# Norm work moved from VectorE to ScalarE and GpSimd, the projection's load on another queue, and a replanned order of the attention stage

## The chip, the cores and the metric

The kernel runs on one core of a Trainium2 chip. Its engines are TensorE (PE, matmuls, with PEld for its weight loads), VectorE (DVE), ScalarE (ACT), GpSimd (POOL) and SyncE (SP, which only issues transfers). ACT and POOL can issue transfers too. Each engine works through its own instructions in order and waits on semaphores for the others. The metric is device time in microseconds (us), the median of several runs; lower is better.

## What is computed

Three stages follow one another. Attention runs over 2 batches of 8 heads, 768 positions and 64 dimensions, with a mask from hash buckets: a query sees the keys whose six projected signs are its own. Its output, as 1536 tokens of 512, goes through a first gated layer of 1536 hidden units behind an RMS norm, and then through a second layer in which each token is sent to one of 8 experts.

```python
q_bits = (np.einsum('bhsd,dk->bhsk', q, proj) > 0)        # k_bits likewise
mask = q_bucket[:, :, :, None] == k_bucket[:, :, None, :]
scores = np.where(mask, scale * np.matmul(q, k.transpose(0, 1, 3, 2)), -1e9)
attn = softmax(scores)
x = np.matmul(attn, v)                                    # to 1536 tokens x 512
rms = np.sqrt(np.mean(x * x, axis=-1, keepdims=True) + 1e-06)
g = (x / rms * rms_g) @ w_gate
x = (silu(g) * ((x / rms * rms_g) @ w_val)) @ w_out
...                                                       # then one of 8 experts per token
```

## The kernel before, in words

**Attention** (to about 232 us of the profiled execution) goes over 8 pairs of heads, i = 0 to 7; j = 0 or 1 is the head in the pair. For each pair the raw k and q are transposed on PE (L660), split into a high and a low half HL (L669 on ACT, L682 on DVE) and projected with PRJ (`ph`, `pb`, L691 and L701). PRJ is made on DVE (step `prj`) from pj, the projection. For each of 12 blocks x of a pair (6 blocks of 128 keys for each head) there are four steps: `sm` on PE (L755) and `sx`, the row maximum on DVE (L763), for the mask; `sc`, the scores on PE (L806); `ex`, the exponential on ACT (L814, tile Pe); `pl`, the low half of it (L825, tile Pl), on POOL or DVE. Then come `pv` (L841 to L843, six query blocks of 18 short matmuls for each head), `pu` (L829, what unmatched queries get, which reads VB and UT, made by POOL at L928 and L780) and `ho` on DVE, three closing steps that write the head's output into X (L852, L856, L858). X holds the tokens, X_71 batch 0 and X_72 batch 1.

The order of all this is written out by hand: ORDER is five strings, one each for PE, ACT, DVE, POOL and SP, in which each word is a step. A class Plan plays the steps, each engine strictly in the order of its string, and gives them their buffers. Other steps stand in the same strings: `iz` clears the operand T of PE's warm-up matmuls (L588; the warm-up, L596, is the first thing PE does, in step `cols`), `rows` writes the mask's constants (L564 to L578), `prz` clears PRJ, `vm1` and `nid` derive small tiles from the identity ident, `z` clears the other T (L600), `n0` to `n5` are the norm of the first chunk and `w0` converts the first weights.

**The first layer** (232 to 560 us) works in three chunks of 512 tokens. Its 36 weight blocks, 12 each of gate (g), value (v) and output (o), come as 64-bit floats. The first chunk converts each of them: loaded into wraw (SP), rebiased on ACT (L439, tile hm), then shift, join and sign on DVE (L443, L447, L455), which gives wy. After that each use needs a high half on ACT (L473: wgh, wvh, woh) and a low half on POOL (L1165) or, for the first two, on DVE (L951). g0 and v0, the first blocks, are converted while attention still runs. A planner with costs orders this stage.

**The norm** of a chunk has 4 sums of squares (L362, 128x512 with an accumulated sum), then 19 operations on 128x4 tiles that find the inverse root (L369 to L392: a shift, a first guess, four Newton rounds of square, times, factor, better), and then the scaling (L399), all on DVE. The norm of chunk 0 runs in attention's pair 5, those of chunks 1 and 2 in the first layer; chunk 1 has tokens of both batches.

## Time and profile before

| | us |
|---|---|
| median of 3 runs | 775.87 |
| lowest, highest | 774.86, 778.15 |
| the profiled execution | 777.31 |
| its span, first to last instruction | 775.6 |

In the profiled execution PE was busy for 735.8 us of the span (95%), DVE for 464.5 (60%), POOL for 427.6 (55%) and ACT for 379.0 (49%). These shares are averages over the three stages, so they are to be read by stretches. In a timeline row the first number is the start in us from the span's beginning, the second the time that the row's instructions took together; brackets give how long the engine was idle before and what it then waited for.

### The profile page before, as it was taken

How to read it: one execution, taken by the hardware profiler on the slowest of the kernel's cores; microseconds unless marked ns; L12 is line 12 of the kernel's file. 1: busy time of each engine (PE TensorE's matmuls, PEld its weight loads, DVE VectorE, ACT ScalarE, POOL GpSimd, SP SyncE). 2: the span in 40 equal slices, each digit the busy share in tenths (PEclk: the TensorE clock that was granted, in tenths of full speed). 3: DMA queues.
4: the chain of work that ended last, by engine and by line, in shares of the span. 5: the costliest groups of instructions: out<-in, count | busy, mean ns of one | idle time of the engine just before them, and what ended most of it. 6: DMA issues, size and time to landing. Idle time of an engine off the chain costs nothing.

```text
span 775.6 us, 14106 instructions
## 1 busy us (share of the span) xinstructions
PE 735.8 (95%) x5349; PEld 618.7 (80%) x5349; DVE 464.5 (60%) x869; ACT 379.0 (49%) x615; POOL 427.6 (55%) x380
## 2 busy tenths in 40 slices
PE   6899999989997999999999999999959999999995
PEld 4678888878885688888887888888858989888894
DVE  5887777889888987786554225422344444464441
ACT  3566356546555444444434443443225666655662
POOL 4889988757773333335434443462155656645552
PEclk9999999999998999999999999999969999999998
DMA  6998785565214344540100010100369997767000
GB/s 130 197 195 171 151 171 116 104 135 116 71 53 139 93 144 144 162 138 27 54 2 1 1 55 0 32 24 0 123 190 326 337 283 225 216 176 180 24 25 21
DMA packets 109193, 92.17 MB, mean 119 GB/s; under 512 B 45663, under 2 KB 90809, under 8 KB 109122
## 3 DMA queue, kind: packets, MB, share of 16 engines
q1 hardware_dynamic: 103930, 82.29, 41.0%
q0 software_dynamic: 2560, 7.34, 3.1%
q10 hardware_dynamic: 2632, 1.60, 1.0%
q8 instruction: 43, 0.70, 0.4%
q14 instruction: 28, 0.23, 0.1%
HBM read 66.36 MB, written 7.36 MB: 95 GB/s over the span
## 4 chain that ended last, share of the span: by engine, by line
PE 83%; DVE 5%; DMA 3%; issue 3%; POOL 2%; ACT 2%; SPq 0%; ACTq 0%; POOLq 0%
PE pg L1146 23%; PE pg L1626 11%; PE pss L806 8%; PE po L1200 4%; PE po L1202 4%; PE po L1201 4%; PE psm L755 4%; PE po L1640 4%; PE po L1638 3%; PE po L1639 3%; PE po L841 2%; PE po L842 2%; PE po L843 2%; PE pt L346 1%; PE pt L660 1%
## 5 line engine op out<-in xcount | busy, mean ns | idle before, releaser
L825 POOL TENSOR_TENSOR Pl<-Pe 128x768 f16<-128x768 f32 x90 | 133.6, 1504 | 33.6 <-ACT Pe L814 31.9
L463 POOL TENSOR_TENSOR wgl<-r,wgh 128x512 fp32r<-128x512 f32 x64 | 83.9, 1317 | 79.6 <-ACT wgh L473 74.1
L814 ACT ACTIVATE Pe<-pss,ebias 128x768 f32<-128x768 f32 x96 | 85.0, 902 | 70.7 <-PE pss L806 49.8
L763 DVE TENSOR_REDUCE m<-psm 128x1 f32<-128x768 f32 x96 | 89.7, 952 | 22.9 <-PE psm L755 21.4
L806 PE MATMUL pss<-T 128*128 128x256 f32 (+1 forms) x384 | 83.9, 351 | 5.3 <-DVE m L763 2.9
L1165 POOL TENSOR_TENSOR wol<-wy_o,woh 128x512 fp32r<-128x512 f32 x36 | 48.4, 1345 | 68.4 <-ACT woh L473 68.4
L1165 POOL TENSOR_TENSOR wgl<-wy_g,wgh 128x512 fp32r<-128x512 f32 x29 | 38.8, 1338 | 78.1 <-ACT wgh L473 70.9
L806 PEld LDWEIGHTS pss<-T 128*128 128x128 f32 x384 | 64.6, 191 | 20.7 <-DVE m L763 3.4
L463 DVE TENSOR_TENSOR wvl<-r,wvh 128x512 fp32r<-128x512 f32 x64 | 47.2, 738 | 48.0 <-ACT wvh L473 45.9
L1626 PE MATMUL pg<-xh,wgh 128*128 128x256 f32 x256 | 73.3, 287 | 0.7 <-ACT xh L349 0.7
L1626 PE MATMUL pg<-xl,wgh 128*128 128x256 f32 x256 | 72.5, 283 | 0.0
L1626 PE MATMUL pg<-xh,wgl 128*128 128x256 f32 x256 | 72.5, 283 | 0.0
L1178 DVE TENSOR_TENSOR si<-pg,si 128x512 f32<-128x512 f32 x30 | 20.7, 688 | 83.1 <-PE pg L1146 83.1
L1146 PE MATMUL pg<-xh,wgh 128*128 128x512 f32 x144 | 58.1, 403 | 4.2 <-ACT wgh L473 3.5
L473 ACT CAST wgh<-r 128x512 fp32r<-128x512 f32 x64 | 39.7, 620 | 42.0 <-PE pg L1626 29.5
L1200 PE MATMUL po<-woh,hh 128*128 128x512 f32 (+1 forms) x148 | 58.8, 398 | 0.5 <-ACT yt L1214 0.5
L841 PE MATMUL po<-VS,Pe 128*128 128x65 f16 x576 | 58.8, 195 | 0.0
L843 PE MATMUL po<-VS,Pl 128*128 128x65 f16 x576 | 57.9, 193 | 0.9 <-POOL Pl L825 0.9
L1146 PE MATMUL pg<-xh,wgl 128*128 128x512 f32 x144 | 57.3, 398 | 1.5 <-POOL wgl L1165 1.2
L842 PE MATMUL po<-VS,Pe 128*128 128x65 f16 x576 | 58.2, 194 | 0.0
L1631 DVE SCALAR_TENSOR_TENSOR ehl<-pg,ehh 128x256 fp32r<-128x256 f32 x64 | 27.1, 424 | 51.6 <-ACT ehh L1630 51.6
L1146 PE MATMUL pg<-xl,wgh 128*128 128x512 f32 x144 | 57.7, 401 | 0.2 <-DVE xl L353 0.2
(260 smaller groups left out, 2021.8 us busy)
## 6 DMA issues: line engine op xcount, KB each, us to landing
r<-in_moe_w_dram SPq DMA_DIRECT2D x128, 256.0 KB
T<-HL SPq DMA_DIRECT2D x44, 384.0 KB
wraw<-in_moe_w_val_dram SPq DMA_DIRECT2D x12, 512.0 KB
wraw<-in_moe_w_gate_dram SPq DMA_DIRECT2D x12, 512.0 KB
wraw<-in_moe_w_out_dram SPq DMA_DIRECT2D x12, 512.0 KB
X<-in_v_dram SPq DMA_DIRECT2D x16, 192.0 KB
y_dram<-yt SPq DMA_DIRECT2D x12, 256.0 KB
kraw<-in_k_dram SPq DMA_DIRECT2D x15, 192.0 KB
```

What stands on the lines that cost most here:

```text
L463: eng.tensor_tensor(out=lo, in0=y, in1=r32(hi), op=ALU.subtract)
L763: v_.tensor_reduce(out=d["m", j][:, t:t + 1], in_=d.pop(("pm", n)), axis=AX.X, op=ALU.max)
L806: nc.tensor.matmul(pss[:, c], Tj[:, a, 0, ks], Tj[:, a, 1, c], start=a == 0, stop=a == 1)
L814: nc.scalar.activation(d["p", j][0][:, kb], d.pop(("s", n)), AF.Exp, bias=ebias, scale=1.0 / math.sqrt(D))
L825: eng.tensor_tensor(out=Pl[:, kb], in0=Pe[:, kb], in1=leading(Pe, kb), op=ALU.subtract)
L841: nc.tensor.matmul(po, leading(Pe, kb)[:, ts], vf[:, 0], start=t == 0 and kb == 0, stop=False, skip_group_check=True)
L842: nc.tensor.matmul(po, leading(Pe, kb)[:, ts], vf[:, 1], start=False, stop=False, skip_group_check=True)
L843: nc.tensor.matmul(po, Pl[:, kb, ts], vf[:, 0], start=False, stop=False, skip_group_check=True)
L1146: nc.tensor.matmul(pg, w_[:, dsl], x_[:, d], start=n == 0, stop=n == 3 * KD - 1)
L1165: nc.gpsimd.tensor_tensor(out=lo, in0=Y[(f, kind)], in1=r32(hi), op=ALU.subtract)
L1200: nc.tensor.matmul(pos[c, t][:, cols], d["hh"][:, tsl], wh[:, cols], start=first, stop=split, skip_group_check=split)
L1626: nc.tensor.matmul(ph, w_[:, dsl], x_[:, d], start=n == 0, stop=n == 3 * KD - 1)
```

## The change

1. `norm_sum`: the sum of squares of each 128x512 tile is an ACT activation (Square with accumulation) in place of a DVE operation; 4 for each of three chunks.
2. `norm_rsqrt`: 14 operations on POOL in place of 19 on DVE. The shift is folded into the guess (a multiplication by -0.5), and there are three Newton rounds in place of four.
3. pj, the projection's load: two transfers of 64x6 from POOL's queue, one ahead of and one behind the mask operation that makes the identity, in place of one of 128x6 from ACT's queue.
4. The first clears on DVE: `iz` first, then `rows`, `prz`, `bc`, `prj`; `vm1` and `nid` behind them.
5. o0 and g1 are also converted while attention runs, as g0 and v0 were (EARLY); the ring of converted weights is two shorter, and wraw and hm have a counted room in the plan.
6. All five strings of ORDER are new.

The diff, cut to its core (of ORDER only the first rows for DVE and POOL are shown):

```diff
-RING = 34
+RING = 32
...
-    "vm1 rows iz nid prz prj td.0.k bc td.0.q bh.0.1.0 bh.0.0.0 bh.0.0.1 bh.0.1.1 sx.0.0 sx.0.5 sx.0.2 sx.0.3 sx.0.1 sx.0.4 vx.0.0 mz.0.0 bi.1 sx.0.6 "
+    "iz rows prz bc prj td.0.k vm1 nid td.0.q bh.0.0.0 bh.0.1.0 bh.0.0.1 bh.0.1.1 sx.0.0 vx.0.0 sx.0.4 sx.0.2 sx.0.3 sx.0.5 sx.0.1 vx.0.2 mz.0.0 bi.1 "
...
-    "z.0.1 c1.0.0.0 ut0 zz z.0.0 z.1.1 z.1.0 c1.0.1.1 sv.0.1 ev.0 c1.0.1.0 c1.0.0.1 sv.0.2 ev.1 const sv.0.0 sv.0.3 pl.0.2 mk.0.0.3 pl.0.0 pl.0.4 pl.0.3 "
+    "pj z.0.1 z.0.0 c1.0.1.0 c1.0.0.1 ut0 c1.0.1.1 zz z.1.0 sv.0.0 sv.0.1 c1.0.0.0 const z.1.1 ev.0 sv.0.2 sv.0.3 pl.0.0 pl.0.3 pl.0.2 pl.0.5 pl.0.4 ev.1 "
...
     def norm_sum(c, i, sq, ss):
         xt = norm_tile(c, i)
-        v_.scalar_tensor_tensor(out=sq, in0=xt, scalar=1.0, in1=xt, op0=ALU.mult, op1=ALU.mult,
-                                accum_out=ss[:, i:i + 1])
+        nc.scalar.activation(sq, xt, AF.Square, accum_out=ss[:, i:i + 1])
 
     def norm_rsqrt(pool, d):
 
         def first():
             d["ms"] = pool.tile([P, CT], F32, name="nms")
-            v_.tensor_scalar(out=d["ms"], in0=d["ss"], scalar1=1.0 / DM, scalar2=1e-6, op0=ALU.mult, op1=ALU.add)
-
-        def half():
-            d["rb"] = pool.tile([P, CT], I32, name="nrb")
-            v_.tensor_scalar(out=d["rb"], in0=d["ms"].bitcast(I32), scalar1=1, scalar2=None, op0=ALU.logical_shift_right)
+            nc.gpsimd.tensor_scalar(out=d["ms"], in0=d["ss"], scalar1=1.0 / DM, scalar2=1e-6, op0=ALU.mult, op1=ALU.add)
 
         def guess():
             d["ri"] = pool.tile([P, CT], F32, name="nri")
-            v_.tensor_scalar(out=d["ri"].bitcast(I32), in0=d["rb"], scalar1=-1.0, scalar2=float(0x5F3759DF),
-                             op0=ALU.mult, op1=ALU.add)
+            nc.gpsimd.tensor_scalar(out=d["ri"].bitcast(I32), in0=d["ms"].bitcast(I32), scalar1=-0.5, scalar2=float(0x5F3759DF),
+                                    op0=ALU.mult, op1=ALU.add)
 
         def square():
             d["t1"] = pool.tile([P, CT], F32, name="nt1")
-            v_.tensor_tensor(out=d["t1"], in0=d["ri"], in1=d["ri"], op=ALU.mult)
+            nc.gpsimd.tensor_tensor(out=d["t1"], in0=d["ri"], in1=d["ri"], op=ALU.mult)
 
         def times():
-            v_.tensor_tensor(out=d["t1"], in0=d["t1"], in1=d["ms"], op=ALU.mult)
+            nc.gpsimd.tensor_tensor(out=d["t1"], in0=d["t1"], in1=d["ms"], op=ALU.mult)
 
         def factor():
-            v_.tensor_scalar(out=d["t1"], in0=d["t1"], scalar1=-0.5, scalar2=1.5, op0=ALU.mult, op1=ALU.add)
+            nc.gpsimd.tensor_scalar(out=d["t1"], in0=d["t1"], scalar1=-0.5, scalar2=1.5, op0=ALU.mult, op1=ALU.add)
 
         def better():
             ro = pool.tile([P, CT], F32, name="nri")
-            v_.tensor_tensor(out=ro, in0=d["ri"], in1=d["t1"], op=ALU.mult)
+            nc.gpsimd.tensor_tensor(out=ro, in0=d["ri"], in1=d["t1"], op=ALU.mult)
             d["ri"] = ro
 
-        return [first, half, guess] + [square, times, factor, better] * 4
+        return [first, guess] + [square, times, factor, better] * 3
 
...
+    EARLY = ((0, "g"), (0, "v"), (0, "o"), (1, "g"))
...
-            if f == 0 and kind != "o":
-                y = wa.tile([P, DM], F32, name=f"wy_{kind}0", bufs=1)
+            if (f, kind) in EARLY:
+                y = wa.tile([P, DM], F32, name=f"wy_{kind}{f}", bufs=1)
             else:
...
-                     "M": 2, "MK": 2}, ORDER)
+                     "M": 2, "MK": 2, "WR": 3, "TMP": 3}, ORDER)
...
         def load_pj():
-            nc.scalar.dma_start(pj[:, 0], proj.unsqueeze(0).to_broadcast((2, D, NB)))
+            for j in range(2):
+                nc.gpsimd.dma_start(pj[64 * j:64 * j + 64, 0], proj)
...
-        add(ACT, 620, "pj", load_pj, (), (), -1999, bw=-1500)
-        add(DVE, 170, "iz", idle_zero, (), (), -1000)
+        add(POOL, 1300, "pj", load_pj, (), (), -1999, bw=-2000)
+        add(DVE, 270, "iz", idle_zero, (), (), -1000)
         add(POOL, 900, "zz", max_zero, (), [("z", 0, 1)], -90)
-        add(DVE, 325, "prz", lambda: v_.memset(r32(PRJ), 0.0), (), (), -98)
+        add(DVE, 485, "prz", lambda: v_.memset(r32(PRJ), 0.0), (), ["iz"], -98)
         add(DVE, 2400, "prj", prj, (), ["pj", "prz"], -97, lock=True)
-        add(DVE, 120, "nid", lambda: v_.tensor_scalar(out=nident, in0=ident, scalar1=-1.0, scalar2=None, op0=ALU.mult), (), (), -90, lock=True)
-        add(DVE, 1200, "rows", mask_rows, (), (), -99)
-        add(PE, 580, "cols", mask_cols, (), ("rows", "iz"), -99, "V")
+        add(DVE, 120, "nid", lambda: v_.tensor_scalar(out=nident, in0=ident, scalar1=-1.0, scalar2=None, op0=ALU.mult), (), ["prj"], -90, lock=True)
+        add(DVE, 1200, "rows", mask_rows, (), ["iz"], -99)
+        add(PE, 1150, "cols", mask_cols, (), ("rows", "iz"), -99, "V")
         add(DVE, 150, "bc", lambda: v_.tensor_copy(bc, st[0].pop("pc")[:, 0:2]), (), ("cols",), -99, "", "V")
...
-            add(DVE, 760, ("n0", i), norm0_sum, (i,), done, N0 + N1 * i, "J", "J", lock=True)
+            add(ACT, 860, ("n0", i), norm0_sum, (i,), done, N0 + N1 * i, "J", "J")
         for n, f in enumerate(steps):
-            add(DVE, 163, ("n1", n), f, (), [("n1", n - 1)] if n else [("n0", i) for i in range(CT)], N0 + N1 * CT, lock=True)
+            add(POOL, 170, ("n1", n), f, (), [("n1", n - 1)] if n else [("n0", i) for i in range(CT)], N0 + N1 * CT)
...
-        for kind in "gv":
-            w = convert(0, kind)
+        for n, (c, kind) in enumerate(((0, "g"), (0, "v"), (0, "o"), (1, "g"))):
+            w = convert(c, kind)
             for m, (e, ns, f, args) in enumerate(((SP, 620, w[0], ()), (ACT, 670, w[1], ()), (DVE, 410, w[2], ()), (DVE, 690, w[3], ()),
-                                                  (DVE, 680, w[4], ()), (ACT, 620, first_hi, kind), (DVE, 690, first_lo, kind))):
-                add(e, ns, ("w0", kind, m), f, args, [("w0", kind, m - 1)] if m else ["next"], NX + (m > 0) * NW, bw=1460 * (m == 0), lock=e == DVE)
+                                                  (DVE, 680, w[4], ()), (ACT, 620, first_hi, kind), (DVE, 690, first_lo, kind))[:7 if n < 2 else 5]):
+                add(e, ns, ("w0", n, m), f, args, [("w0", n, m - 1)] if m else ["next"], NX + (m > 0) * NW + n,
+                    ("WR", "TMP", "", "", "", "", "")[m], "WR TMP" if m == 4 else "", bw=2100 * (m == 0), lock=e == DVE)
         plan.emit()
 
...
-                    if c == 0 and not w0:
+                    if c == 0 and (f, kind) not in EARLY:
...
-                    add(DVE, 680, ("M.n0", c + 1, i), sums, (), prev.get("ns") or [("M.next",)], nat - NL + 0.2 * i, "TMP", "TMP", lock=True)
+                    add(ACT, 860, ("M.n0", c + 1, i), sums, (), prev.get("ns") or [("M.next",)], nat - NL + 0.2 * i, "TMP", "TMP")
                 steps = norm_rsqrt(wa, d)
                 for n, fn in enumerate(steps):
-                    add(DVE, 163, ("M.n1", c + 1, n), fn, (), [("M.n1", c + 1, n - 1)] if n else [("M.n0", c + 1, i) for i in range(CT)],
-                        nat - NL + 1, lock=True)
+                    add(POOL, 170, ("M.n1", c + 1, n), fn, (), [("M.n1", c + 1, n - 1)] if n else [("M.n0", c + 1, i) for i in range(CT)],
+                        nat - NL + 1)
                 for i in range(CT):
```

**DVE near 155 us.** The rows are DVE's in pair 5 of attention. L362 to L392 are the norm of chunk 0, L763 are row maxima, mT and UT are small masks, den and rd closing steps of a head. Before:

```order
L369 TENSOR_SCALAR nms<-nss 128x4
L773 TENSOR_SCALAR mT<-pT 6x128
L763 TENSOR_REDUCE m<-psm 128x1
L373 TENSOR_SCALAR nrb<-nms 128x4
L763 TENSOR_REDUCE m<-psm 128x1 x2
L777 TENSOR_SCALAR UT_127<-pT 6x128
L377 TENSOR_SCALAR nri<-nrb 128x4
L763 TENSOR_REDUCE m<-psm 128x1
L852 TENSOR_SCALAR den<-po,vsc_147 128x6
L382 TENSOR_TENSOR nt_2630<-nri 128x4
L763 TENSOR_REDUCE m<-psm 128x1
```

The same part of the program after (L758 are the row maxima, L847, L851 and L853 the closing steps):

```order
L768 TENSOR_SCALAR mT<-pT 6x128
L758 TENSOR_REDUCE m<-psm 128x1 x5
L847 TENSOR_SCALAR den<-po,vsc_146 128x6
L758 TENSOR_REDUCE m<-psm 128x1
L851 RECIPROCAL rd<-den 128x6
L853 TENSOR_TENSOR X_71<-po,rd 128x6x64
L768 TENSOR_SCALAR mT<-pT 6x128
L758 TENSOR_REDUCE m<-psm 128x1
L772 TENSOR_SCALAR UT_126<-pT 6x128
L758 TENSOR_REDUCE m<-psm 128x1
```

The operations L369, L373, L377 and L382 that stood between row maxima are not in DVE's rows of attention any more.

**PE at the end of attention.** The rows are PE's around `pu.7.0` (L829 before, L824 after). Before, all of head 7.0's matmuls and half of head 7.1's stood ahead of it, and head 7.1's others behind:

```order
L842 MATMUL po<-VS_124,Pe 128x65
L843 LDWEIGHTS Pl
L843 MATMUL po<-VS_124,Pl 128x65
L829 LDWEIGHTS UT_127
L829 MATMUL po<-VB_130,UT_127 128x390
L841 LDWEIGHTS Pe
L841 MATMUL po<-VS_124,Pe 128x65
L842 LDWEIGHTS Pe
L842 MATMUL po<-VS_124,Pe 128x65
```

After, the matmuls ahead of it are the last of head 7.0, and those behind the first of head 7.1:

```order
L837 MATMUL po<-VS_124,Pe 128x65
L838 LDWEIGHTS Pl
L838 MATMUL po<-VS_124,Pl 128x65
L824 LDWEIGHTS UT_127
L824 MATMUL po<-VB_130,UT_127 128x390
L801 MATMUL pss<-T_122 128x512 x2
L801 MATMUL pss<-T_122 128x256 x2
L836 LDWEIGHTS Pe
L836 MATMUL po<-VS_124,Pe 128x65
L837 LDWEIGHTS Pe
L837 MATMUL po<-VS_124,Pe 128x65
```

The score matmuls of block 7.8 (L801), which stood ahead of all of head 7.0's short matmuls, now stand between `pu.7.0` and the first short matmul of head 7.1.

**ACT at the start of the first layer.** L439 (L433 after) rebiases, L473 (L467 after) makes a weight's high half, L1174 (L1170 after) is the gate's activation. The first wgh and wvh are those of g0 and v0, woh is o0's, the second wgh g1's. Before:

```order
L814 ACTIVATE Pe<-pss,ebias 128x768 x9
L473 CAST wgh<-wy_g_3628 128x512
L814 ACTIVATE Pe<-pss,ebias 128x768
L473 CAST wvh<-wy_v_3899 128x512
L439 ACTIVATE hm<-wraw 128x512 x3
L473 CAST woh<-wy_o 128x512
L1174 ACT_TABLE_LOAD
L1174 ACTIVATE si<-pg 128x512
L439 ACTIVATE hm<-wraw 128x512
L473 CAST wgh<-wy_g 128x512
```

After:

```order
L809 ACTIVATE Pe<-pss,ebias 128x768 x4
L433 ACTIVATE hm<-wraw 128x512
L467 CAST wgh<-wy_g_3870 128x512
L467 CAST wvh<-wy_v_3634 128x512
L360 ACTIVATE sq,nss<-X_71 128x512 x2
L360 ACTIVATE sq,nss<-X_72 128x512 x2
L433 ACTIVATE hm<-wraw 128x512 x2
L467 CAST woh<-wy_o_3953 128x512
L433 ACTIVATE hm<-wraw 128x512
L467 CAST wgh<-wy_g_3977 128x512
```

Four sums of squares (L360) and two rebias steps stand ahead of woh of o0 and wgh of g1; the ones with X_72 read the last head's output. The rebias steps of o0 and g1 moved ahead of the end of attention.

## Rows read from the trace of the kernel before

**Rows 1.** Windows: length, busy us of PE, PEld, DVE, ACT, POOL; PE clock, DMA, GB/s.
```profile
35.00:155.00 120.00, 119.15 (x1448) 101.03 (x1447) 94.52 (x149) 69.53 (x86) 104.61 (x92) 1.00 0.77 153
155.00:165.00 10.00, 7.06 (x60) 5.74 (x60) 8.27 (x14) 3.40 (x4) 4.27 (x3) 0.83 0.96 206
...
220.00:232.40 12.40, 10.61 (x234) 9.28 (x232) 10.25 (x12) 6.03 (x9) 8.72 (x7) 1.00 0.20 63
232.40:275.70 43.30, 37.18 (x149) 27.70 (x149) 39.91 (x77) 19.89 (x33) 13.62 (x14) 0.92 0.36 114
275.70:560.00 284.30, 283.31 (x1352) 233.76 (x1350) 143.96 (x260) 116.80 (x199) 117.13 (x87) 1.00 0.19 60
```

**Rows 2.** Timeline of the first 18 us: start, us, engine, line, operation, [idle before].
```profile
4.84 1.89 PE L596 MATMUL pc<-T 128*128 128x512 bf16 x4 [4.84 <-DVE T L588]
...
5.33 0.16 DVE L552 TENSOR_SCALAR pj<-pj 128x6 f32<-128x6 f32 x2
...
7.67 0.17 DVE L561 TENSOR_TENSOR PRJ<-pj,PRJ 64x6 fp32r<-64x6 f32 x1
...
12.98 2.75 PE L701 MATMUL pd<-HL,PRJ 128*128 128x512 f32 x12
```

**Rows 3.** One line, L1607, the transfers that POOL issues: ns min/median/max.
```profile
L1607 POOL DMA_INDIRECT yg<-y_dram,gid x16: 992/1005/1284, 565.9 to 666.1; - x16
...
DMA to landing us min/median/max: 3.4/4.1/9.4
```

**Rows 4.** Timeline from 148 to 166 us, three engines.
```profile
154.96 4.31 POOL L825 TENSOR_TENSOR Pl<-Pe 128x768 f16<-128x768 f32 x3
...
155.23 4.07 DVE L377 TENSOR_SCALAR nri<-nrb 128x4 int32<-128x4 int32 x1
...
160.21 2.93 PE L806 MATMUL pss<-T 128*128 128x512 f32 x8 [2.94 <-DVE m L763]
```

**Rows 5.** Windows behind the waits near 157 and 239 us, columns as in rows 1.
```profile
159.80:163.20 3.40, 2.99 (x9) 2.60 (x10) 2.12 (x7) 0.92 (x2) 0.00 (x0) 0.50 1.00 216
241.70:248.50 6.80, 5.88 (x13) 4.19 (x14) 6.80 (x15) 1.64 (x3) 3.10 (x2) 0.50 0.70 226
```

**Rows 6.** One line, L763, the row maxima: ns min/median/max.
```profile
L763 DVE TENSOR_REDUCE m<-psm x96: 935/957/959, 19.7 to 209.1; 128x1 f32<-128x768 f32 x96
```

**Rows 7.** Lines L868 and L309, operations near those that move.
```profile
L868 ACT ACTIVATE junk<-X x8: 834/846/850, 15.0 to 64.3; 128x768 f32<-128x768 f32 x8
L868 ACT ACTIVATION_READ_ACCUMULATOR junk<-X x8: 183/186/191, 15.7 to 65.0; 128x1 f32 x8
...
L309 POOL CAST ecol<-iota_i x1: 190/190/190, 27.3 to 27.3; 128x8 f32<-128x8 int32 x1
```

**Rows 8.** Timeline of the tail of attention, POOL and DVE.
```profile
228.10 1.27 POOL L928 TENSOR_TENSOR VB<-VM,diag 38x384 f16<-38x384 f16 x1
...
223.14 1.54 DVE L825 TENSOR_TENSOR Pl<-Pe 128x768 f16<-128x768 f32 x1 [0.64 <-ACT Pe L814]
...
230.50 0.23 DVE L852 TENSOR_SCALAR den<-po,vsc 128x6 f32<-128x6 f32 x1 [0.58 <-PE po L829]
...
230.99 0.56 DVE L858 TENSOR_TENSOR X<-po,rd 128x384 f32<-128x384 f32 x1
```

**Rows 9.** The crossing, 232.4 to 275.7: ACT's timeline, PE's waits, DVE's lines.
```profile
234.81 1.34 ACT L439 ACTIVATE hm<-wraw 128x512 f32<-128x512 f32 x2 [3.64 <-DVE sq L362]
...
241.55 0.60 ACT L473 CAST wgh<-wy_g 128x512 fp32r<-128x512 f32 x1
...
PE pg L1146 <- ACT wgh L473: 3.5, 1, 3.5
...
L443 DVE TENSOR_SCALAR hm<-hm 128x512 uint32<-128x512 uint32 x12 | 4.9, 418 | 0.9 <-ACT hm L439 0.9
...
L455 DVE SCALAR_TENSOR_TENSOR wy_o<-wraw,hm 128x512 uint32<-128x512 uint32 x4 | 2.7, 687 | 0.0
```

More of the change, by code (lines that the diff above doesn't have):

```diff
@@ L970, in attention @@
             add(POOL, 180, ("ev", i), ends_V, (i,), ["prj"], -98)
-        add(DVE, 800, "vm1", ends_VB, (), (), -89, lock=True)
+        add(DVE, 800, "vm1", ends_VB, (), ["prj"], -89, lock=True)
         add(POOL, 400, "ut0", zero_UT, (), ["prj"], -98)
@@ L1488, in first_layer @@
                         ready = [("M.cv", f, kind, 4)]
+                    done = ("M.next",) if (f, kind) in EARLY else ("M.cv", f, kind, 4)
                     pr = (at if kind != "o" else yat) - WL + (0.3, 0.4, 0.8)[n]
@@ L1491, in first_layer @@
                     if not w0 and not (shared and c):
-                        ready = ready or ([("M.cv", f, kind, 4)] if f or kind == "o" else [("M.next",)])
+                        ready = ready or [done]
                         add(ACT, 620, ("M.hi", c, f, kind), weight_hi, (c, f, kind), ready + prev.get(kind, []), pr,
```

106 rows, old and new, of the table ORDER are left out of this document.

## The prediction

> **What bounds the kernel now.** I read the busy time of each engine by stretches first, then the timeline where TensorE (PE) is short of work. In the stretches [rows 1] the reader is to see where PE is not full. From 35 to 155 us it works 119.15 of 120, from 275.7 to 560 it works 283.31 of 284.3: there PE is the bound, and freeing another engine gives nothing. The second MoE behind 560 us keeps its instructions and its inputs' layout; I cost it at nothing. What is left to win lies in four short places: the first microseconds, 155 to 165 us (7.06 of 10), the tail of attention (10.61 of 12.4) and the crossing into the first MoE (37.18 of 43.3).
>
> At the start [rows 2], PE's first matmuls begin at 4.84 and say themselves what they waited for: the clear of T on VectorE (DVE), line L588, which stands behind the constants of the mask and many small clears. PE then takes its work in order: more warm-up, the transposes of k, and the projection (L701) at 12.98. The projection also needs PRJ, which DVE makes from pj between 5.33 and 7.84.
>
> At 155 us [rows 4], one 128x4 operation of the norm (L377, which takes 0.16 us elsewhere) lasts 4.07, from 155.23 to 159.30, while GpSimd (POOL) runs three Pl subtractions from 154.96 to 159.27. The row maximum L763 queued behind it, and PE idled 2.94 for that maximum. Right behind that wait the granted clock is 0.50 of full, the lower of the two levels (1.2 GHz), for 3.4 us; behind the wait at 242 us it is the same for 6.8 us [rows 5].
>
> In the crossing PE waits 3.5 us for the high half of weight g1 (L473 on ScalarE, ACT) [rows 9]. The rebias that feeds it began at 234.81, held up 3.64 us by DVE's norm sums (line L362, tile sq), and the cast itself came at 241.55.
>
> **Start: -3.3.** With T's clear first on DVE, PE begins about 0.4 after DVE's first operation at 0.89, near 1.3 instead of 4.84: 3.5 earlier, and what follows in order with it. The projection's turn then comes near 9.5, so PRJ must be done by then and pj landed by about 7.0 (PRJ takes 2.5 [rows 2]). pj now comes over POOL's queue in two transfers. The nearest POOL transfers in the trace [rows 3] take 1.0 us each to issue and land 3.4 to 9.4 (middle 4.1) after. The second is issued behind the first and behind the identity's mask, near 2.3, and lands at 5.7 to 6.4 by the low and middle figures: in time. At 9.4 it lands at 11.7, PRJ is done at 14.2 and the projection is 1.3 later than before. Both ends, -3.5 and +1.3, go into the range; I take -3.3, by the middle of the row, since these transfers are smaller than the gathers. T's other clears and the rest of the constants stay off this path.
>
> **Norm off DVE: -4.0.** The four sums and 19 small operations of the first norm leave DVE's queue, so no 128x4 operation stands between row maxima while Pl runs. That takes away the 2.94 idle and, if the clock stays up, half of the 2.99 that PE worked at the lower level [rows 4, 5]: 2.94 + 1.50 = 4.4. I keep 0.4 for small waits. Could another DVE operation take the stall's place? L763 itself ran 96 times at 0.935 to 0.959 [rows 6], Pl beside it or not; operations that read SBUF can be held, so nothing gained is the other end. The work that arrives elsewhere: a square with accumulation on ACT, by the nearest rows [rows 7] at most 0.84 + 0.19 for 768 columns, 0.86 scaled to 512, four of them 3.4 us; 14 POOL operations of about 0.19 (a 128x8 cast there), 2.7 us. In attention these lie beside other work: POOL has 15.4 us free of 120 and ACT more.
>
> The lock between these two engines has a rule in the Trainium skill ("SBUF — State Buffer", SBUF: two separate sides): a shared port pair is held exclusively for a whole instruction and the loser blocks. The trace agrees that L377 was released when the third Pl ended, within 0.03 us, after three of them and not one. By the rule taken alone a move from DVE to POOL cures this stall, but lets DVE's two-input operations wait 14 times for a short POOL operation, at most 14 x 0.19 = 2.7 us of DVE time that PE need not feel; the sum would go from -4.0 to -1.3.
>
> **Tail of attention: +1.5.** In the new PE order the last head's score block sc.7.8 comes behind pu.7.0, directly ahead of pv.7.1.0, and DVE has the closing steps of head 7.0 and two Pl ahead of what pv.7.1.0 needs. Counted from the end of pu.7.0 [rows 8]: 0.58 to the first closing step, 1.05 to the end of the third (230.50 to 231.55), two Pl at 1.54: 4.7 us. PE fills 0.75 of it with the scores (four of the eight matmuls that took 2.93 at the lower clock [rows 4]). So it idles up to 3.9; with Pl at 0.9 apiece, 2.6. Against that, the 1.8 idle of this stretch [rows 1] goes, since VB of the last pair (1.27, between the last Pl and PE's pu.7.0 [rows 8]) now stands ahead. Net +0.8 to +2.1; I take +1.5. The bounds: -1.8 with no new wait, +3.6 if the clock falls behind it as it did behind the 2.94 and the 3.5 (1.5 more, as at 159.8).
>
> **Crossing: -3.0.** o0 and g1 are now rebiased in attention, and this chunk's norm leaves DVE. But ACT's queue holds four sums ahead of two rebias steps, woh of o0, another rebias and then wgh of g1, and the last two sums read the last head's output. That output is late too: behind the last Pl, DVE has g0's and o0's remaining conversion (0.42 and 0.69 apiece [rows 9]), interleaved with the closing steps. From the end of the last Pl I count two operations of 0.42, seven of 0.69 and the three closing steps (0.23, about 0.2, 0.56 [rows 8]): 6.7 us. PE needs 3.8 from there to the end of attention (108 of the 218 short matmuls in the tail's stretch [rows 1], whose 10.61 less 16 score matmuls of 0.18 is 7.7). So the output comes 2.9 after attention's last matmul, and then ACT needs 1.7 for two sums, 1.34 for two rebias steps [rows 9], 0.6, 0.7 and 0.6: g1 is ready 7.8 after attention. Before, it was 9.8 (241.55 + 0.60, less 232.4), and PE asked for it 3.5 sooner, at 6.3. So about 1.5 of the wait stays: -2.0. DVE being freer should take another 1.0 of the 2.6 us of smaller idle in this stretch (43.3 less 37.18 is 6.1 idle, of which 3.5 is this wait). I leave the clock as before here. The bounds are 0 (the rebias steps ahead wait for their weights' transfers) and -9.0 (all 6.1 idle gone, and half of the 5.88 at the lower clock).
>
> **Elsewhere: 0.** Chunk 2's norm lies in the stretch where PE is full; the cover is 284 us of matmuls, with POOL at 117 and ACT at 117 of 284. The rest of attention is replanned, but PE has only 0.85 idle in 120 to lose; what it could cost is a rival below.
>
> The sum is -3.3 - 4.0 + 1.5 - 3.0 = -8.8 against the profiled execution's 777.31 (span 775.6): 768.5. That execution lay 1.4 above the median of the runs, 775.87, so I say 767.0.
>
> **Rivals.**
> *pj late.* If the POOL transfers land like the slowest gather, start is +1.3 instead of -3.3: 771.6. For it: two 64-row transfers on a queue that first has to be fed by POOL, with DVE busy clearing from 0.9 on. Against: the middle landing is 4.1. A rule that speaks for this case stands in the same page and section (the "DVE blocks DMA" box): a transfer issued on the POOL queue needs GpSimd to write its descriptors and starves while DVE holds the shared port. No row of before shows a transfer on that queue beside DVE clears. Chance 0.11.
>
> *The waits stay and the clock falls.* Tail at +3.6 and the stall only moved to another DVE operation: up to 767 + 2.1 + 4 = 773. For it: both long PE waits of before are followed by the lower clock. Against: L763 was never stretched. Chance 0.14.
>
> *Better.* The crossing's wait shrinks under what lowers the clock: up to 6 more, 757 to 763. For it: 2.9 us of the crossing's loss is clock alone. Against: the late head output above. Chance 0.16.
>
> *Slower.* Pl on POOL becomes late for pv all through attention. Place: POOL, 104.61 busy of 120 before, Pl at 1.44 us [rows 1, 4], with the norm's operations now put between Pl of pair 5, and moved VB. If PE waits w more per head over the 14 heads ahead of the last pair, the sum is spent at 8.8 / 14 = 0.63 us a head, and slower by 0.5% from 12.7 / 14 = 0.91: 780 and up. For it: POOL is the fullest engine beside PE. Against: the new order keeps at least 3.6 us of PE work between a head's last scores and its first pv, which is what exp and Pl take, before the last head. Chance 0.07, half of it within 0.5% of before.
>
> **How the numbers follow.** The forecast, 763 to 770, has 0.52. A measurement of this kernel tells about 0.5% (3.9 us) from no change, so faster means under 772. Faster: 0.52 + 0.16, 0.07 of pj late, 0.08 of the waits, together 0.83; the same 0.04 + 0.05 + 0.03 = 0.12; slower 0.05. The range 757 to 774 leaves out the slower rival and some of each end, under 2 in 10.
>
> **What would show it.** PE's first matmul near 1.3 and the projection near 9.5 show the start right; PRJ's steps beginning after 7 show pj late. No DVE operation of 4 us near 155 and clock 1.00 there show the norm's term; a PE wait of 2.5 to 4 us for Pl before the last head's pv shows the tail's, and a wait of about 2 for wgh of g1, the crossing's. I am wrong if PE waits for Pl in the middle of attention, or if PE waits less than 1 us at g1.

## The result and the profile after

The changed kernel takes 765.38 us in the median of its first four runs (763.95 to 769.72) against 776.42 for the kernel before in the same comparison: a ratio of 0.9869, 95% interval 0.9842 to 0.9895. The forecast was 767.0 in a range of 757 to 774. Run again on another occasion (e1 below) it took 766.74 against 776.73, ratio 0.9869 (0.9844 to 0.9894).

The first profiled execution was the slowest of the four, 769.72, so the rows below are from the second profile, e1 (765.49, span 763.8), unless said otherwise. Windows, columns as in [rows 1]; the stretches are cut at the same places of the program, which now come earlier:

```profile
5.00:35.00 30.00, 23.70 (x120) 17.26 (x120) 24.78 (x56) 15.79 (x24) 21.90 (x45) 1.00 0.99 190
35.00:150.00 115.00, 113.86 (x1395) 97.46 (x1394) 86.72 (x137) 67.89 (x91) 102.72 (x93) 1.00 0.80 160
150.00:160.00 10.00, 10.00 (x141) 8.63 (x141) 6.83 (x10) 5.15 (x7) 9.41 (x18) 1.00 0.32 57
160.00:210.00 50.00, 50.00 (x694) 43.73 (x691) 40.24 (x63) 29.55 (x37) 41.57 (x36) 1.00 0.44 102
210.00:223.50 13.50, 11.96 (x243) 10.63 (x241) 9.69 (x19) 8.70 (x14) 6.26 (x5) 1.00 0.18 64
223.50:264.00 40.50, 35.18 (x146) 27.57 (x146) 32.72 (x48) 22.34 (x44) 20.91 (x30) 0.92 0.39 120
264.00:548.00 284.00, 282.86 (x1357) 234.58 (x1356) 132.78 (x235) 117.15 (x200) 121.38 (x98) 1.00 0.19 61
```

The stretch that held the stall is full now: 10.00 of 10.00 at a clock of 1.00, where [rows 1] had 7.06 of 10 at 0.83. The planned first layer is as full as before (282.86 of 284.0). The crossing is still not full, 35.18 of 40.5 at 0.92.

The step `pu` ends each head on PE, so its 16 starts measure how far ahead the changed kernel is. Against the profile before, it leads by 3.6 us at `pu.4.0` (152.83 against 156.39), by 7.2 at the next head (166.14 against 173.35), by 7.8 at `pu.6.1`, by 9.0 at `pu.7.1` (223.13 against 232.16) and by 11.8 at the end of the span. Read as they stand, these leads give 3.6 for the start, 3.6 for the stall, 0.6 for the rest of attention up to its tail, 1.2 for the tail and 2.8 for what follows.

But the two orders of PE don't have the same work ahead of each `pu`. Ahead of `pu.4.0` the old order has the scores of one more block (`sc.5.0`), ahead of `pu.6.1` the new order has one more (`sc.7.2`). A block of scores takes about 0.76 us (16 such matmuls, four blocks, took 3.05 in e1). With that put right, the start is worth about 2.8, the stall 4.4, the rest 1.4 and the tail 0.4; mask blocks that also changed places, about 0.4 us each, are left out. The idle time of PE in the tail agrees: 1.79 before (220.00 to 232.40 in [rows 1]) and 1.54 in e1 (210.00 to 223.50 above).

### The profile page after: what moved, and what is told of

The parts are those of the page before. It is cut to its first block, busy times and chain, and to the rows that moved or that the text cites. A ratio compares the mean times of both kernels' runs of the same rounds, so it can differ in the third digit from the quotient of the medians.

```text
span 768.0 us, 14078 instructions
## 1 busy us (share of the span) xinstructions
PE 730.5 (95%) x5349; PEld 619.3 (81%) x5349; DVE 430.8 (56%) x788; ACT 384.4 (50%) x639; POOL 443.4 (58%) x424
## 4 chain that ended last, share of the span: by engine, by line
PE 85%; DMA 5%; DVE 4%; issue 2%; POOL 1%; ACT 1%; ACTq 1%; POOLq 0%; DVEq 0%
PE pg L1142 25%; PE pg L1623 11%; PE pss L801 8%; PE psm L750 4%; PE po L1196 4%; PE po L1198 4%; PE po L1197 4%; PE po L1635 3%; PE po L1637 3%; PE po L1636 3%; DMA T<-bits 3%; PE po L836 2%; PE po L837 2%; PE po L838 2%; PE pd L686 2%
## 5 line engine op out<-in xcount | busy, mean ns | idle before, releaser
L758 DVE TENSOR_REDUCE m<-psm 128x1 f32<-128x768 f32 x96 | 90.0, 953 | 27.3 <-PE psm L750 25.3
L801 PE MATMUL pss<-T 128*128 128x256 f32 (+1 forms) x384 | 81.1, 347 | 0.9 <-DVE T L792 0.5
L801 PEld LDWEIGHTS pss<-T 128*128 128x128 f32 x384 | 64.2, 191 | 14.6 <-ACT Pe L809 1.5
L1623 PE MATMUL pg<-xh,wgh 128*128 128x256 f32 x256 | 73.9, 289 | 0.7 <-ACT xh L347 0.7
L1623 PE MATMUL pg<-xl,wgh 128*128 128x256 f32 x256 | 73.5, 287 | 0.0
L1623 PE MATMUL pg<-xh,wgl 128*128 128x256 f32 x256 | 73.3, 286 | 0.0
L1174 DVE TENSOR_TENSOR si<-pg,si 128x512 f32<-128x512 f32 x30 | 20.6, 687 | 87.4 <-PE pg L1142 84.1
L467 ACT CAST wgh<-r 128x512 fp32r<-128x512 f32 x64 | 39.6, 619 | 43.4 <-PE pg L1623 29.4
L750 PE MATMUL psm<-T 128*128 128x512 f32 x192 | 52.9, 367 | 6.0 <-DMA T<-bits 3.8
L1161 POOL TENSOR_TENSOR wvl<-wy_v,wvh 128x512 fp32r<-128x512 f32 x29 | 39.6, 1367 | 31.8 <-ACT wvh L467 30.5
```

Source lines behind the costliest of these rows:

```text
L750: nc.tensor.matmul(pm[:, c], Tj[:, 0, 1, t * P:(t + 1) * P], Tj[:, 0, 0, c], start=True, stop=True)
L758: v_.tensor_reduce(out=d["m", j][:, t:t + 1], in_=d.pop(("pm", n)), axis=AX.X, op=ALU.max)
L801: nc.tensor.matmul(pss[:, c], Tj[:, a, 0, ks], Tj[:, a, 1, c], start=a == 0, stop=a == 1)
L1161: nc.gpsimd.tensor_tensor(out=lo, in0=Y[(f, kind)], in1=r32(hi), op=ALU.subtract)
L1623: nc.tensor.matmul(ph, w_[:, dsl], x_[:, d], start=n == 0, stop=n == 3 * KD - 1)
```

## The experiments

All comparisons are of medians; the kernel before was run beside each.

| run | what | median, us | ratio to before (95%) |
|---|---|---|---|
| e1 | changed kernel again | 766.74 | 0.9869 (0.9844 to 0.9894) |
| e2 | changed, g1's cast first | 763.98 | 0.9841 (0.9822 to 0.9860) |
| e3 | changed, pj on ACT's queue | 766.78 | 0.9878 (0.9858 to 0.9897) |
| e4 | before, sums and roots moved | 770.29 | 0.9909 (0.9893 to 0.9926) |
| e5 | before, clears reordered | 774.73 | 0.9973 (0.9955 to 0.9991) |
| e6 | changed, o0 and g1 not early | 766.58 | 0.9857 (0.9831 to 0.9883) |
| e7 | changed, last VB behind the last Pl | 768.53 | 0.9894 (0.9865 to 0.9923) |
| e8 | e2, and Pl of 7.6 earlier | 762.90 | 0.9818 (0.9791 to 0.9846) |
| e9 | before, roots moved alone | 771.07 | 0.9930 (0.9903 to 0.9956) |
| e10 | before, sums moved alone | 778.35 | 1.0035 (1.0015 to 1.0055) |
| e11 | e8, pair 0's transfers first | 763.66 | 0.9830 (0.9807 to 0.9854) |

**The changed kernel again (e1).** 

> The changed kernel once more, for a second profile. The first profiled execution was 769.72, the slowest of four (763.95, 764.5, 766.26). Theory A (three local repairs: the stall at 155, the tail, the crossing; the start's 3.5 is given back in pair 0, whose first masks wait for transfers): the time is 764 to 766 and in the profile the end of attention lies 5 to 9 earlier than the 232.2 of before, the crossing 2 to 3 shorter; the 2.9 us wait of PE for T<-bits at 35 us is there or not, and its size is what differs between executions. Rival B (the start is what gained, the rest is noise): PE is 3 us ahead from pair 0 on in this profile.

The median, 766.74, is a little above theory A's 764 to 766; attention ends 9.0 earlier, as the 5 to 9 of the theory allow, and the part behind it is 2.8 shorter. The lead is -0.1 at `pu.0.0`, where the new order has already done two blocks of scores more, and 3.1 at `pu.1.1`, about what rival B said of this profile; that the rest is noise is refuted by the leads at 155 us and behind. The 2.88 us wait of the first profile (first row below) is absent from this one, and the stretch around it differs as the next two rows show: first profile, then e1.

```profile
35.59 0.98 PE L750 MATMUL psm<-T 128*128 128x512 f32 x2 [2.88 <-DMA T<-bits]
```
```profile
25.00:37.00 12.00, 7.87 (x37) 6.03 (x38) 8.93 (x13) 5.42 (x9) 10.97 (x22) 0.93 0.95 138
```
```profile
25.00:37.00 12.00, 9.57 (x51) 7.19 (x50) 10.39 (x19) 7.23 (x10) 11.32 (x22) 1.00 1.00 186
```

In the first profile the transfers of the second pair's masks came late (138 GB/s against 186 in the same stretch), and `pu.4.0` stood at 156.33, level with before. That is 3.5 of the 4.2 us between the two spans; the rest of these two executions is nearly alike. PE's start itself is the same in both.

**Which part of the norm's move matters (e4, e9, e10).** All three are the kernel before. e4 takes parts 1 and 2 of the change, e9 part 2 alone, e10 part 1 alone. The functions are as in the change's diff; in ORDER the steps of chunk 0 move to their new engine's string at the same place:

```diff
-    "... ho.3.1.2 n0.3 n0.2 bi.6 n0.0 sx.5.4 n0.1 n1.0 mk.5.0.1 ..."        # DVE
+    "... n0.0 n0.1 ex.4.11 vs.5.0 n0.2 ex.4.9 n0.3 d1.6.0 ..."               # ACT (e4, e10)
+    "n1.0 n1.1 pl.5.0 n1.2 pl.5.5 n1.3 pl.5.4 n1.4 pl.5.2 n1.5 pl.5.3 ..."   # POOL (e4, e9)
```

> The kernel before with the first two parts of the change alone: sums on ScalarE, roots on GpSimd, the steps of chunk 0 moved to these queues at the same place of attention, all else in the order of before. Theory A (the stall at 155 is worth 3.7, the norm in the crossing some more): 771 to 773, no operation of 4 us on VectorE, PE without its 2.94 wait. Rival (the replanned order as a whole brings the gain; the stall only moves to another operation of VectorE): 775 to 777.

> The kernel before with the roots alone on GpSimd (14 operations in place of 19 on VectorE), the sums still on VectorE. Theory A (the stall at 155 is a root operation held behind three Pl, so the roots carry all of it): 771 to 773, PE without its 2.94 wait. Rival (the sums' 3.1 us on VectorE are as much of it): 774 to 775.

> The kernel before with the sums alone on ScalarE, the 19 root operations still on VectorE. Theory A: the roots still stand between row maxima with Pl running beside them, so a stall of 3 to 4 us of PE stays near 155, and only the crossing gains: 775 to 777. Rival (which operation meets the Pl is chance, and the move of the sums alone shifts it away): 772 to 773.

e4 is 6.4 us faster than before, e9 5.0 faster, e10 2.3 slower. PE's order is that of before in all three, so the stretch from `pu.4.0` to `pu.4.1` can be compared as it is. Before, e9 and e10 (e4's row has the same 12.63 of 12.63 as e9's):

```profile
156.39:173.35 16.96, 14.02 (x161) 11.95 (x160) 13.35 (x27) 8.31 (x10) 7.76 (x7) 0.90 0.60 129
```
```profile
154.60:167.23 12.63, 12.63 (x161) 10.83 (x161) 7.79 (x12) 8.21 (x10) 8.68 (x13) 1.00 0.81 174
```
```profile
155.25:173.45 18.20, 15.32 (x162) 13.05 (x161) 13.30 (x27) 8.31 (x10) 7.71 (x6) 0.81 0.56 120
```

Without the roots on DVE the stretch is 4.3 shorter, 2.9 of it idle time and 1.4 time at the lower clock. In e9's profile PE's 2.94 wait is gone and the lead grows from 1.8 at `pu.4.0` to 6.1 at the next head; in e10 it shrinks from 1.1 to -0.1, and the stall is there again. DVE's lines from 140 to 175 us in e10 (busy us, mean ns), and its two rows in time, DVE's and POOL's:

```profile
L376 DVE TENSOR_SCALAR nri<-nrb 128x4 int32<-128x4 int32 x1 | 4.0, 4008 | 0.0
```
```profile
154.09 4.01 DVE L376 TENSOR_SCALAR nri<-nrb 128x4 int32<-128x4 int32 x1
```
```profile
153.76 4.31 POOL L824 TENSOR_TENSOR Pl<-Pe 128x768 f16<-128x768 f32 x3
```

L376 is L377 of before. It begins 0.33 after the first of three Pl and ends with the third, at 158.10 and 158.07. So the same small operation is caught again when the sums are gone, and no longer exists on DVE when the roots are gone. The roots carry most of the gain of parts 1 and 2. Moving the sums too adds 0.8 (771.07 to 770.29) or, each against its own runs of the kernel before, 1.5; the intervals of the two ratios overlap. The rival that the stall only moves to another DVE operation is refuted: in e4 none of DVE's lines from 140 to 175 us has a mean over 1.08 us. e10's 778.35 is over the 775 to 777 of its theory A: the stall stayed, as it said, but the crossing gained nothing (from `pu.7.1` to the end of the span 543.5 us, 543.4 before; the wait for wgh is 3.9), and the lower clock behind the stall cost 1.2 more than in the profile before. How much of the 2.3 is the sums' move itself is not shown, since the planner placed the first layer anew. e4's 770.29 is 0.7 under the range of its theory.

**The clears alone (e5).**

```diff
-    "vm1 rows iz nid prz prj td.0.k bc
+    "iz rows prz prj vm1 nid td.0.k bc
```

> The kernel before with the order of the first clears alone: iz, rows, prz, prj, then vm1 and nid; pj as before, on ScalarE's queue. Theory A (PE starts 3.5 earlier and keeps it, less what pair 0's transfers T<-bits take back, which differs between executions): 773 to 775 as a median, 1.5 to 3.5 faster, with the first warm-up at 1.3. Rival (pair 0 is bound by its transfers, so an earlier PE only waits longer there): 776 to 777, no change.

774.73: 1.75 faster, the edge of theory A. In its profile the lead is 3.4 us from `pu.1.1` on and stays so to `pu.4.0`. But e4, e9 and e10, whose start is that of the kernel before, led that same profile by 0.9 to 1.8 at `pu.4.0`: the profile before had itself a slow start, and the typical gain of the start is nearer to 2 than to 3.5. The start of the profile says why it is not 3.5: the first matmul comes at 1.31 here too, but PE then waits 0.94 for kraw, and the projection begins at 10.63, which is 2.35 earlier than before and not 3.5. e5's own 12 runs spread from 772.49 to 777.64, more than the 2.7 us of e4's six.

**pj's queue (e3).** load_pj and its step as in the kernel before, with `pj` first in ACT's string.

> The changed kernel with pj loaded as before: one transfer, first on ScalarE's queue. Theory A (over GpSimd's queue pj landed at 7.6 and held the first projection until 10.7, where its turn was near 9.5): PRJ is ready before PE asks, the projection begins 1 to 1.5 earlier, and the kernel is 0 to 1.5 faster, 763 to 765. Rival (the earlier queue delays the second head's k, which then is what PE waits for): 0 to 1 slower, 765 to 766.

766.78, equal to e1 (766.74) and above both ranges that were expected. The rows of the start show the trade. In e1 pj landed for DVE's first step at 7.33, and the projection (L696) waited for PRJ; second, the same place in e3's waits:

```profile
1.31 1.89 PE L591 MATMUL pc<-T 128*128 128x512 bf16 x4 [1.31 <-DVE T L583]
...
2.48 0.58 POOL L543 DMA_DIRECT2D pj<-in_proj_dram  x1
...
7.33 0.25 DVE L547 TENSOR_SCALAR pj<-pj 128x6 f32<-128x6 f32 x2 [2.99 <-DMA pj<-in_proj_dram]
...
10.42 0.94 PE L696 MATMUL pd<-HL,PRJ 128*128 128x512 f32 x4 [1.76 <-DVE PRJ L555]
```
```profile
PE psm L749 <- ACT Pe L808: 1.6, 1, 1.6
...
PE psm L749 <- DMA T<-bits: 1.2, 1, 1.2
PE pt L654 <- DMA kraw<-in_k_dram: 1.0, 1, 1.0
```

With pj on ACT's queue PE no longer waits for PRJ, but 1.0 for kraw, issued behind pj, and 1.2 for the masks' transfers. The projection begins at 10.65, in e1 at 10.42. Neither queue wins.

**Early conversion (e6).** Only g0 and v0 in EARLY, the words w0.2 and w0.3 out of ORDER, the ring at 34:

```diff
-    EARLY = ((0, "g"), (0, "v"), (0, "o"), (1, "g"))
+    EARLY = ((0, "g"), (0, "v"))
```

> The changed kernel without the early conversion of o0 and g1: both are converted in the first layer again, the ring has 34 slots, the rest of attention's order is the same. Theory A (the early conversion is worth about a microsecond, since g1's cast waits for its place in ScalarE's queue anyway; most of the crossing's 2.8 comes from the norm's move): 0.5 to 2 slower than the changed kernel, 767 to 768. Rival (the early conversion is what shortened the crossing): 2.5 to 4 slower, 769 or more.

766.58, no different from the changed kernel and faster than both expectations: part 5 is worth nothing that these runs can tell. PE's wait for wgh is 2.2 here, 2.6 in e1. The planner also put two of the four sums earlier, at 205 us among the exponentials (in e1 they run from 221.92 on), so this run does not price the conversion alone.

**The tail (e7).** VB of the last pair goes behind the last Pl on POOL again:

```diff
-    "... pl.5.10 vb.7.0 pl.6.0 ... mk.6.1.3 vb.7.1 pl.6.6 ... pl.7.3 mk.7.1.3 pl.7.7 pl.7.11 pl.7.9",
+    "... pl.5.10 pl.6.0 ... mk.6.1.3 pl.6.6 ... pl.7.3 pl.7.7 pl.7.11 pl.7.9 vb.7.0 vb.7.1 mk.7.1.3",
```

> The changed kernel with VB of the last pair behind the last Pl on GpSimd again, as before, and the tail's PE order as changed. Theory A (the tail gained 1.2 where 1.5 of loss was predicted since VB and UT no longer stand behind the last Pl): head 7.0's closing then waits for VB, which ends 1.5 to 2 after the last Pl of GpSimd, and the two Pl on VectorE and head 7.1 come later by that: 1 to 2 slower, 767 to 768.5. Rival (the tail gained because Pl on VectorE took 0.91 and not 1.54): within 0.5 of the changed kernel.

768.53, 1.8 slower: theory A, at the upper end of its range; the spreads of these six runs and of e1's overlap. PE's waits from 208 to 300 us in e7 (for what, us in total, times, the longest):

```profile
PE pg L1142 <- POOL wgl L1161: 2.8, 2, 2.4
PE po L824 <- POOL VB L923: 2.2, 1, 2.2
PE po L838 <- DVE Pl L820: 1.5, 2, 1.0
...
PE pg L1142 <- ACT wgh L467: 0.5, 1, 0.5
```

The wait for VB is new, 2.2; the wait for Pl is the same 1.5 in e1, so it has nothing to do with VB. In this profile the tail is 3.7 longer than in e1, more than the wait: behind `pu.7.0` the granted clock was 0.78, and the same work took 1.4 more. The rows are from `pu.7.0` to `pu.7.1` in e1, in e7 and in e6:

```profile
216.75:223.13 6.38, 4.84 (x116) 4.24 (x113) 5.94 (x12) 3.68 (x7) 1.41 (x1) 1.00 0.16 46
```
```profile
220.38:228.18 7.80, 6.25 (x114) 5.58 (x113) 6.40 (x12) 3.96 (x8) 1.01 (x2) 0.78 0.28 81
```
```profile
217.21:225.07 7.86, 6.32 (x116) 5.72 (x114) 4.01 (x7) 2.04 (x3) 1.41 (x1) 0.78 0.23 69
```

e6 has no wait for VB and the same two waits for Pl as e1, and still fell to 0.78 there, so the clock's fall is not shown to come from the VB wait. Note also the last row of the waits: when attention ends later, the wait at g1 shrinks from 2.6 to 0.5, since g1's readiness does not come earlier with PE. Part of what the tail gains is handed over to that wait.

**The crossing (e2).** One cast is moved forward in the planner's order:

```diff
-                    pr = (at if kind != "o" else yat) - WL + (0.3, 0.4, 0.8)[n]
+                    pr = (at if kind != "o" else yat) - WL + (0.3, 0.4, 0.8)[n] - 1.5 * (c == 0 and (f, kind) == (1, "g"))
```

> The changed kernel with one cast moved: the high half of g1 stands right behind the four sums in ScalarE's queue, ahead of two rebias steps, of woh of o0 and of the rebias that waits for its transfer. Theory A (the 2.4 us wait for wgh at 233 is a matter of the queue's order, and the lower clock behind it follows from it): g1's wait falls from 2.4 under 0.5, the clock stays at 1.00 through the crossing, 3 to 5 us faster than the changed kernel, about 760. Rival: GpSimd's norm operations and wol take the place (wgl late) and no more than 1 us is gained, 764 to 765.

ACT's timeline at the crossing, e1 first, e2 second:

```profile
226.13 0.62 ACT L360 ACTIVATE sq<-X 128x512 f32<-128x512 f32 x1
...
227.85 0.61 ACT L467 CAST woh<-wy_o 128x512 fp32r<-128x512 f32 x1
230.48 0.67 ACT L433 ACTIVATE hm<-wraw 128x512 f32<-128x512 f32 x1 [2.02 <-DMA wraw<-in_moe_w_gate_dram]
231.05 0.60 ACT L467 CAST wgh<-wy_g 128x512 fp32r<-128x512 f32 x1
```
```profile
227.69 0.62 ACT L360 ACTIVATE sq<-X 128x512 f32<-128x512 f32 x1
...
228.30 0.61 ACT L467 CAST wgh<-wy_g 128x512 fp32r<-128x512 f32 x1
...
231.30 0.66 ACT L433 ACTIVATE hm<-wraw 128x512 f32<-128x512 f32 x1 [0.76 <-DMA wraw<-in_moe_w_gate_dram]
```

In e1 ACT sits for 2.02 us on the rebias of a later weight whose transfer has not landed, with g1's cast queued behind it. In e2 the cast is done 0.6 behind the sums; no wait of PE for wgh is listed any more. What replaces it is smaller, 1.3 for wvh and 0.7 for wvl of v1. Windows of 223.5 to 264 us: e1's row stands above (35.18 busy of 40.5, clock 0.92), e2's is

```profile
223.50:264.00 40.50, 36.73 (x193) 29.03 (x190) 34.95 (x51) 25.61 (x51) 22.67 (x31) 0.96 0.44 140
```

The median is 2.8 under e1's, a little short of the 3 to 5 of theory A (763.98, where it said about 760). The two profiles are 1.9 apart although e2's attention ended 1.6 later (`pu.7.1` at 224.69 against 223.13), so what follows attention is 3.5 shorter in this pair. Other profiles with the same first layer make that less sure. From `pu.7.1` to the first gate matmul of the second layer (L1623, in e3 L1622) it takes 339.0 us in e1, but 338.7 in the first profile of the changed kernel and 337.2 in e3; with g1's cast first it takes 335.9 in e2, 335.5 in e8 and 336.4 in e11. The gain is there in every pair, and lies between 0.8 and 3.5. Part of the difference is the clock, which fell for a different length in executions of one and the same program. The same window in e3, to be compared with e1's 0.92, and in e8, to be compared with e2's 0.96:

```profile
223.50:264.00 40.50, 35.85 (x158) 27.89 (x155) 33.63 (x49) 24.05 (x48) 20.97 (x31) 0.96 0.42 130
```
```profile
223.50:264.00 40.50, 36.46 (x170) 28.12 (x167) 36.02 (x52) 25.14 (x49) 24.27 (x32) 1.00 0.46 151
```

That the lower clock follows from the wait for wgh, as theory A has it, is not shown: e2 has no such wait and fell all the same.

**A faster version (e8) and a miss (e11).** e8 is e2 with one word moved in DVE's string, e11 is e8 with SyncE's string changed:

```diff
-    "... pl.7.10 ho.7.0.0 ho.7.0.1 ho.7.0.2 pl.7.6 pl.7.8 ..."     # e8, DVE
+    "... pl.7.10 pl.7.6 ho.7.0.0 ho.7.0.1 ho.7.0.2 pl.7.8 ..."
-    "... lv.1 e2.0.0 l.2.q lv.2 d1.0.1.0 d0.1.0 lv.3 ..."           # e11, SP
+    "... lv.1 e2.0.0 d1.0.1.0 d0.1.0 l.2.q lv.2 lv.3 ..."
```

> The kernel of the earlier run with g1's cast first, and one more step moved: Pl of block 7.6 on VectorE goes ahead of the closing steps of head 7.0 instead of behind them. Theory A (PE's 1.5 us wait for Pl in the tail is a matter of VectorE's order): the wait falls to 0.5 or less, 0.7 to 1 faster than g1 first alone, 763. Rival (the closing of head 7.0 comes later and with it nothing is gained, since the wait is for block 7.8): 764.

> The previous kernel (g1 first, Pl of 7.6 early) with one more edit in SyncE's order: pair 0's transfers d1.0.1.0 (T<-bits) and d0.1.0 (T<-HL) go ahead of pair 2's loads of q and v instead of behind them. Theory A (in pair 0 PE waits for these transfers because the loads' traffic stands ahead of them): the end of pair 0 comes 0.5 to 2 earlier and the median falls to 761 to 762.5. Rival (the wait is for the later T<-bits of pair 1 and the v loads are needed as early): unchanged or up to 2 slower, 763 to 765.

e8 takes 762.90, 1.1 under e2, the fastest measured. PE's wait for Pl fell from 1.5 to 0.8, and a wait of 0.8 for Pe, hidden before, came up. The tail as a whole got no shorter. From `pu.6.1` to `pu.7.1`, e2 and then e8:

```profile
210.97:224.69 13.72, 12.18 (x245) 10.82 (x243) 9.53 (x19) 8.46 (x13) 6.84 (x5) 1.00 0.18 58
```
```profile
210.04:223.76 13.72, 12.18 (x246) 10.83 (x243) 10.80 (x19) 8.46 (x13) 7.55 (x5) 1.00 0.20 58
```

So one wait took the place of the other, as the rival has it in kind, and the word that moved does not explain the 1.1. In the profiles e8 is ahead by 0.9 before it reaches the tail; the spreads of the two, 763.56 to 766.25 and 761.76 to 764.64, overlap.

e11 takes 763.66, inside its rival's 763 to 765. `pu.0.0` comes at 56.17, in e8 at 54.97; other profiles of this start lie between 54.88 and 58.82. Nothing is gained by these two transfers that these runs can tell. What holds up the second pair's masks in the longer executions stays open.

## Why the prediction was right, point by point

**The total.** -8.8 forecast; measured -11.0 by the medians of the first comparison and -10.0 in e1. By medians the parts add up: norm -6.4 (e4), clears -1.75 (e5), VB ahead -1.8 (e7), early weights and pj's queue 0 (e6, e3), together -9.95. That the parts add so closely is luck: each of them is uncertain by about 1 us or more, and e7 shows that tail and crossing trade with each other. No run has the new strings of ORDER with the norm and the start of before, so what the rest of the replanning is worth is known only as the remainder, about 2 to 3. The misses of single steps offset each other in part: the start gave less than forecast, the stall and the tail gave more.

**Start, -3.3: mechanism right, size too large.** PE began at 1.31, as forecast. But the second pj transfer, issued at 2.48, let DVE begin at 7.33 and not at 6.4 or before; by the prediction's own sign (PRJ's steps after 7) pj was late. PRJ took 3.1 and not 2.5, since one of its steps was stretched to 0.76: it began at 8.22 and ended 0.03 after a cast on POOL (8.13 to 8.95). PE reached the projection 1.8 early and waited. I took the middle landing of the gathers, 4.1, where it was 4.85, nearer to the middle than to the 9.4 of the rival. The step that was mis-sized is "3.5 earlier, and what follows in order with it": the projection came not 3.5 but 2.3 to 2.6 earlier (12.98 before, 10.42 in e1, 10.65 in e3, 10.63 in e5), and with pj on ACT's queue it was kraw that was not there. Behind that, pair 0's transfers give back more in some executions. By e5, which leaves pj's queue as before, the start is worth 1.75; in e1's profile it is 2.8.

**Norm, -4.0: right.** The stall is worth 4.3 between two heads in e4 and e9, where I had 4.4 before the 0.4 for small waits. The new operations cost what the neighbouring rows said: a sum on ACT 0.63 + 0.19, a root operation on POOL 0.19 to 0.20 where nothing disturbs it. (My 0.86 for a sum does not follow from the row it names, which scaled to 512 columns gives 0.75.) The row maxima kept their 0.96. The rule of the Trainium skill ("SBUF — State Buffer", SBUF: two separate sides) that one engine holds the shared port pair for a whole instruction agrees with e10 in the end of the wait, where L376 ended with the third Pl to 0.03 us; that the wait went on through three of them is more than the rule says. Its other half, DVE held up by the 14 short operations, cost PE nothing that shows: 10.00 busy of 10.00, and 50.00 of 50.00 behind it.

**Tail, +1.5: wrong in sign.** The tail became about 0.4 shorter where 1.5 longer was forecast. I counted 0.58 to the first closing step and 1.54 for each of two Pl. In e1 it was 0.03 (`pu.7.0` ends at 217.09, the row below begins at 217.12) and 0.95 (1.82 for the two), and PE waited 1.5 in two pieces, not 2.6 to 3.9:

```profile
217.12 0.23 DVE L847 TENSOR_SCALAR den<-po,vsc 128x6 f32<-128x6 f32 x1 [1.72 <-PE po L824]
...
218.08 1.82 DVE L820 TENSOR_TENSOR Pl<-Pe 128x768 f16<-128x768 f32 x2
```
```profile
215.21 2.95 POOL L820 TENSOR_TENSOR Pl<-Pe 128x768 f16<-128x768 f32 x2 [0.62 <-ACT Pe L809]
```

Both prices could have been read from the trace of the kernel before:

```profile
230.13 0.34 PE L829 MATMUL po<-VB,UT 38*128 38x390 f16 x1 [0.62 <-POOL UT L780]
```
```profile
219.46 2.70 DVE L825 TENSOR_TENSOR Pl<-Pe 128x768 f16<-128x768 f32 x3 [0.20 <-ACT Pe L814]
```
```profile
222.39 5.75 POOL L825 TENSOR_TENSOR Pl<-Pe 128x768 f16<-128x768 f32 x3 [2.95 <-ACT Pe L814]
```

`pu.7.0` ended there at 230.47, and the first closing step began at 230.50 [rows 8]: also 0.03. The 0.58 in that row's brackets is how long DVE had been idle, not the distance from `pu.7.0`. The 1.54 of [rows 8] was measured while POOL ran its own Pl from 222.39 to 228.14; three Pl on DVE ahead of that, from 219.46 on, when POOL had finished its own at 219.44, took 2.70 together, 0.9 apiece. In the new order POOL has finished at 218.16, so the quiet price holds. I had used a duration from a stretch in which two engines were in each other's way for one in which they are not. The gain I counted against it, VB ahead, was right in kind; e7 puts it at 2.2 of PE wait.

**Crossing, -3.0: right in size, half right in cause.** -2.8 between the profiles, with 2.6 of the g1 wait left where I said 1.5. I held the four sums and the late head output responsible. The sums ended sooner than I said (226.84, 3.4 behind attention's end, against 2.9 + 1.7); what kept g1 was the rebias with its 2.02 us for a transfer, which I had named only as a bound. g1 was ready 8.2 behind attention's end, not 7.8, and PE asked at 5.7, not 6.3. The gain seems to come from the norm's move and not from the early weights: from `pu.7.1` to the first gate matmul of the second layer it takes 342.6 us before (341.5 in e5, whose first layer is the same), 338.7 in e4 with the weights as before, 338.6 in e6 and 339.0 in e1. Roots alone (e9, 341.1) and sums alone (e10, 342.9) bring little of it. Each of these is one execution, and executions of one program differ by up to 1.8 here.

**The rivals.** pj was late, by 0.9 to 1.6 us against my 5.7 to 6.4, and not by 5. Of the waits that stay, the stall is gone; in the crossing the clock fell to 0.50 for about as long in e1 as before. The slower rival did not come: from 35 to 210 us PE is idle 1.1 of 175, and no wait for Pl is among its waits between 60 and 208 us.

## What to carry to other kernels

Look for the small operation that sits in a queue between two others that someone waits for: a 0.16 us step that can be held for 4 us costs what it blocks, and the place to move it is decided by who is behind it, not by the engine's share of busy time. When a duration is taken from a row for a new order, check what the neighbouring engine did during that row; a row measured under contention over-prices the same work in a quiet place. The bracket of a timeline row says how long that engine was idle, not how long after its releaser it began. A wait that gets smaller in a list is not yet time gained: compare the stretch between two fixed steps, and see that both orders have the same work in it. In an in-order queue, put a cast whose input is ready ahead of a step that waits for a transfer.
